# Where the weights and the rest of x are loaded around the last inverse transform: first layer's weights early, second layer's weights and x later

## The chip, the cores and the metric

The kernel runs on one core of a Trainium2 chip. The metric is the device time of one launch in microseconds (us), as the median of several runs.

A core has five engines that take their instructions from queues of their own: PE (TensorE, matmul), DVE (VectorE), ACT (ScalarE), POOL (GpSimd) and SP (SyncE, which here only issues DMAs). They meet at semaphores. Each works through its queue in order: an instruction that waits holds up everything behind it on that engine, and nothing on another one that doesn't ask for it.

## The reference

One block of a transformer with adaptive layer norm. The sequence has 2048 positions of 640 channels, everything in bf16. It is

```python
mod = (_silu(c) @ w_mod).reshape(c.shape[0], 6, 1, -1)      # sa, ca, ga, sb, cb, gb
h = _layernorm(x) * (1 + ca) + sa
x = x + ga * A(h, k, v, shift_k, ssm_k, ssm_D)              # A: q * (fftconv(shift(k) * v, ssm_k) + ...)
h = _layernorm(x) * (1 + cb) + sb
x = x + gb * B(h, w1, w2, w3, w4)
# B: h1  = gelu(layernorm(h) @ w1), its four channel quarters moved by 1, -1, 2, -2 positions
#    x1  = h + h1 @ w2
#    out = x1 + gelu(layernorm(x1) @ w3) @ w4
```

A is a long convolution over the sequence, written in the reference with a real FFT of 4096 points. w1 and w2 are 640 x 640, w3 is 640 x 1728 and w4 1728 x 640.

## The kernel before

**Stages.** The FFT is done as matmuls with tables of sines and cosines that the kernel makes itself. `stage1` and `stage2_half` transform first ssm_k and then k * v. `inverse1` (ten blocks, `h` 0 to 1 and `b` 0 to 4) multiplies the two spectra on DVE (line 678), with the real and imaginary halves of one of them swapped by a DMA beforehand (line 674), and does the first half of the way back on PE (lines 689 and 690). `inverse2` does the second half, for two or three tiles of 128 positions at a time: 32 small matmuls of 32 rows by 32 columns for each tile (line 722), then two casts from PSUM to `y_all` in the buffer `Rb` (lines 211 on ACT and 213 on DVE). There are 16 tiles, in the calls [0, 1, 2], [3, 4], [5, 6, 7], [8, 9, 10], [11, 12, 13], [14, 15]. The order of the calls on PE is not the order of the tiles.

The convolution part mixes channels and positions in such a way that all of `inverse1` must be done before `inverse2` can start. From there the work goes tile by tile:

- `chain_a` (lines 798 to 801, `square_sum` at 790 on ACT) multiplies y by the gate q, adds x and sums for the layer norm; `ln_finish` (lines 763 to 779) makes mean and reciprocal root on POOL and DVE; `chain_b` (lines 812 to 817) applies the second modulation and sums again; `chain_c` (line 785 or 655) normalises for w1, and `turn` transposes on PE (line 829) and copies back from PSUM on ACT or DVE (lines 835 and 837).
- `mm_w1` multiplies by w1 (line 875 on PE, gelu at 877 on ACT), and by 128 of its columns that were gathered in `w1x` (885, gelu at 891).
- `mm_w2` (930, addition 937 on DVE), `mm_w3` (967 and 971, gelu 978 and 980), `mm_w4` (997 and 1006, then 1029 to 1035 on DVE and the store at 1038).

The first three tiles go alone through this (`CG = [[0], [1], [2], [3, 4], ...]`), the others two by two.

`make_q` (lines 655 to 663) makes q from the layer norm of x; `ln1_stats` (600 and 601 on DVE, 608 and 609 on ACT) and `ln1_fin` (618 to 623 on POOL) its statistics. x is loaded by `x_load` (line 587), four DMAs for each group of tiles: tiles 0 to 7 early, tiles 8 to 11 and 12 to 15 in the part that is changed. `mod_half` (549, 555, 562 to 570) makes the six modulation vectors from w_mod, one half vector at a time, each with a load of 400 KB, five matmuls and one copy.

**Memory.** Buffers are used several times. The table `Gs` of the transform lies in columns 0 to 6143 of `RG`. When `stage2_half` has done its last matmul, `w1_sb` takes columns 0 to 3199, `w2_sb` 3200 to 6399 and `w1x` 6400 to 7039. Columns 6144 to 8191 are also one of the four places for the swapped spectrum (`KSY`), last used by the ninth block of `inverse1`. x's tiles 8 to 15 go to the upper half of `Ra`, which is free long before. w3 and w4 go to `T01`, which the matmuls of `inverse2` read to the end.

**Order.** Every piece of work is added to a `Planner` as a task with the regions that it reads and writes, from which its dependences follow. The costs given there have no effect any more: the list `ORDER`, written out at the top, says in which order the tasks are issued, on which engine each runs (the letter: P, A, D, G for POOL, S) and which of the four PSUM places it gets (behind the colon). A task's number is the order in which `add` was called.

**What the waits of before are.** After the first call of `inverse2` stands

```python
y0 = [("Rb", 0, D)]
```

and w1, w2 and the eight x loads all read this region: they wait for the casts of tiles 0 to 2 although they need nothing of them. For w2 there is a POOL copy of one element from tile 0 of y into `w2_sb` (line 1061) that comes first; its four pieces of 32 rows for each quarter (line 1065) and its main part (1063) then wait for this copy. The copy into `w1x` (1066, POOL) waits for w1.

In SP's queue of before, the first piece of w2 stands first and waits for the POOL copy; then an x load, the last load of w_mod, w1, three x loads, w2, and the rest. Behind these stand w3 (1082) and w4 (1079, 1080, 1084).

Of the kernel before, what the change touches and what calls it, by code (L numbers as in the profile page):

```python
# [15 lines left out]
S, D, F = 2048, 640, 1728  # L16
P = 128
NT = S // P
# [9 lines left out]
38G 88P:0 90P:1 89A 17P:2 70D 122S 71D 13G 106P:3 91A 33S 84P:0 18A 107A 74G 56G 86P:2 57G 66D 85A 75D 119S 96P:3 49G 87A 98P:0 102P:1 67D 128S 99A  # L28
125S 117P:2 103A 39G 123P:0 118D 97A 137S 82P:1 58G 131S 124D 112P:2 83A 104P:3 113D 110P:0 105A 78P:1 111D 92P:2 40A 120P:3 93A 41G 129P:0 121D 134S
79A 65G 76P:2 130D 126P:3 77A 114P:1 127D 150S 80P:0 115A 232S 100P:2 42D 138P:3 43D 101A 140P:1 139D 44A 52D 45A 51D 132P:3 81A 47S 46G 135P:2 133D  # L30
35S 53A 94P:0 54A 156S 59D 146P:3 95A 55G 153S 136D 159S 141D 108P:0 221P:2 147D 109A 142P:1 60A 222A 61D 48S 205P:3 143D 162S 199P:0 62G 206A 203P:2
200A 187P:3 204D 151P:1 188A 197P:0 63G 152D 165S 219P:2 198A 230S 201P:3 220D 223P:1 229S 202A 185P:0 224D 144P:2 186A 227P:0 145D 209P:1 228A 154P:3
210A 225P:0 155D 168S 215P:2 226A 191P:1 216D 157P:3 192A 160P:0 171S 158D 189P:2 231S 166P:1 161D 190A 211P:3 167D 207P:0 212A 148P:2 208D 64A 250S
213P:0 149D 163P:3 214A 195P:1 164D 217P:2 196A 169P:0 218D 193P:3 170A 172P:1 194D 174P:2 247S 173A 236D 366S 367G 239A 244S 176P:1 175D 234A 184D
182P:2 235A 177D 286P:3 178P:0 287A 183D 238A 278D 288P:3 284P:2 180P:1 289A 179D 285A 292P:3 181D 294P:0 293A 282P:2 295A 279D 251P:3 248P:1 283A
259S 296P:0 256S 249A 281D 290P:2 297A 245P:1 291A 300P:0 253S 280D 246A 316P:2 301A 298P:1 317A 320P:0 252D 299A 321D 308P:2 314P:3 309A 318P:1 315D
306P:0 383G 257P:2 307A 233D 272S 276G 319A 342P:0 273G 258D 275S 332P:3 343D 237G 324P:2 382S 333A 338P:1 325D 270S 328P:0 339A 277S 254P:3 274S 329A
326P:2 255D 269G 267S 340P:1 327D 263G 322P:3 266S 341A 262G 334P:0 271S 268G 323D 312P:2 335A 264S 240G 260P:1 265S 474D 313A 310P:3 465D 374S 302P:0
261D 311A 304P:2 471D 303D 336P:1 305A 375G 330P:3 337D 391G 390S 331A 348P:2 360P:0 349A 472D 356P:3 368D 352P:1 357A 358P:2 369D 353A 364P:3 361A
365D 362P:1 398S 399G 376D 359A 344P:3 370P:0 363A 466D 449S 372P:2 377D 371A 346P:1 385D 345A 406S 407G 380P:0 373A 378P:3 384D 414S 415G 381A 354P:2  # L40
393D 347A 388P:0 392D 422S 423G 355A 386P:1 379A 473D 394P:2 401D 387A 350P:3 400D 430S 431G 351A 396P:1 395A 475D 404P:3 409D 397A 402P:2 408D 438S
439G 405A 446S 417D 389A 452S 410P:1 403A 412P:3 416D 411A 450P:0 425D 420P:2 413A 424D 418P:1 421A 433D 458S 419A 426P:3 455S 428P:2 241A 432D 464G
451D 436P:1 427A 441D 447P:0 429A 440D 434P:3 437A 242D 442P:2 435A 444P:1 467D 243G 443A 477D 468D 453P:3 478D 445A 448D 456P:2 479D 454A 480P:10
469D 457A 476D 470D 518P:23 481A 482D 514G 520A 537D 511P:01 483G 538D 486S 519A 493S 558D 540G 539A 578D 461S 559D 484S 459P:2 513A 495S 579D 541G
512A 491S 524P:13 561D 460A 542D 494S 560A 515P:20 485S 563D 580A 487S 562G 581D 489S 525A 606D 543D 497S 550A 582G 564D 544A 545D 565A 609D 546G 566D
526A 583D 488S 462P:1 517A 551D 498S 567G 584D 496S 516A 547D 607D 585A 548P:0 490G 586D 549A 610D 608A 587G 553P:0 568D 611A 612D 463D 569P:2 554A
588D 613G 570D 589P:1 552D 521P:23 571D 590D 618A 555P:0 614D 535S 596P:1 556A 619D 532S 615D 530S 620D 597A 594P:0 492S 616D 531S 621A 576P:1 572D
529S 622D 617A 527S 573D 528S 595A 523D 623G 577A 534S 574P:0 533S 669D 672D 624A 627D 670D 536S 575A 628P:1 625P:3 629A 673D 598P:0 671A 626D 675G
674A 638P:3 599D 636P:1 639A 676G 601D 500D 600A 677D 681D 637A 602G 682D 683D 522A 643P:1 603D 684A 678D 604P:2 679D 640P:3 605A 644D 680A 685G
660P:2 641D 645A 686G 658P:1 661A 646D 642A 656P:2 687D 659A 690D 647G 499A 591D 688P:1 691P:3 689D 654P:0 692D 657A 648D 501G 651D 701P:3 655A 592D  # L50
652P:2 506A 649P:1 653D 699P:0 650D 505D 702A 593D 507G 630D 717P:1 631D 700A 739D 740D 503A 633D 703P:0 632D 742D 741A 743D 706P:3 718A 745D 744A
634D 723P:1 707D 502A 746G 662P:2 704D 709G 751D 708A 752D 705A 635D 753D 724A 710G 747A 754A 721P:1 663D 504G 508A 711D 714D 809D 748D 712P:2 763A
715P:0 719P:3 716D 722A 749D 713A 664D 750A 793P:2 764D 666S 693A 755D 668S 765D 789P:1 665S 756G 794A 694D 667S 509A 695D 812D 813D 791P:2 790A 510G
760D 810D 814A 815D 761P:1 792A 787P:0 762D 757D 720A 833D 834D 811A 882D 758P:3 883D 725P:21 696A 816G 759D 884A 697D 788A 698D 879D 821A 766D 880D
817A 822D 885G 771P:0 823D 769P:3 772A 818D 819D 824A 825D 726P 835D 820A 727D 881A 767D 826G 728D 770A 729S 731S 886G 827A 776P:3 732S 733D 730S 830A
768D 946D 828P:1 831P:2 777D 829A 773P:0 887A 832D 734D 841P:2 839P:3 836D 738S 842A 943D 736S 774D 737S 888D 779G 775A 944D 795P:20 891A 947D 778A
889D 948A 892D 780G 893D 840A 949D 895D 796P 781A 797D 945A 798D 890A 950G 784D 802S 894A 735S 799S 785P:2 896G 803D 782P:3 786A 843P:1 837D 783A 955D
557G 951A 804D 846P:3 956D 808S 844D 806S 861P:2 805S 847D 845A 800S 838D 848A 897D 1007D 857P:3 862A 952D 1008D 900A 1010G 849G 901P:2 898P:1 902D
863P:0 899A 953D 1009A 957D 905P:1 954A 903P:2 1011G 864A 906A 959G 1012D 1013D 859P:0 1014D 904A 850G 1016D 858A 910P:2 860A 958A 907P:0 911D 960G
851D 912A 865P:23 908D 854A 913D 909A 1015A 914G 1017G 855P:0 852P:1 856A 866P 918D 964D 853D 867D 915D 868D 871S 916P:2 921P:1 872S 917D 869S 1018D  # L60
# [4 lines left out]
1040P:0 997S 1002D 1069A 1005S 1003S 1098P:2 1041A 1004S 1042P:1 939S 1076P:0 1046P:3 1077A 1043A 1044P:0 1072P:1 1045A 1047A 1048P:30 1073A 1049P  # L65
1050D 1074P:3 1056D 1057D 1051D 1060S 1092P:0 1075A 1052S 1070P:1 1099A 1054S 1059S 1053S 1058S 1006S 1094P:2 1071A 1055S 1061S 1096P:3 1095A 1093A
1078P:21 1097A 1079P 1080D 1081D 1082S 1085S 1084S 1083S 1100P:23 1086D 1087D 1101P 1088S 1104D 1091S 1105D 1089S 1108S 1090S 1110D 1109S 1111D 1107S
1113A 1114S 1115A 1112S 1106S
"""


# [69 lines left out]
def kernel(  # L141
# [4 lines left out]
    nc = tc.nc  # L146
# [928 lines left out]
    for tl in rest:  # L1075
        inverse2(tl)
# [68 lines left out]
```

## Time and profile before

| what | value |
|---|---|
| median of 3 runs | 314.64 us (314.64, 314.64, 319.94) |
| profiled execution, its own time | 316.53 us |
| its span, first to last instruction | 314.8 us |
| busy: PE, PEld, DVE, ACT, POOL | 286.4, 222.4, 226.7, 229.7, 102.0 us |
| mean granted clock of PE | 0.966 |
| DMA moved | 32.20 MB |
| w1 (L1062), 800 KB | issued at 112.57 us, landed 7.2 us later |
| w2 (L1063), 640 KB | issued at 114.61 us, landed 9.4 us later |
| L1061, the POOL copy | 110.66 us |
| first matmul of `inverse2` (L722) / `mm_w1` (L875) / `mm_w2` (L930) / `mm_w3` (L971) | 108.44 / 124.71 / 137.47 / 147.21 us |

A line of the profile gives, from the left: start and duration in us, engine, line of the kernel, operation, output tile and input tiles, shape, count; in square brackets the idle time of the engine in front of it and what ended it. "issue" means that nothing the profile shows was waited for. Such an attribution names the latest event among those that the instruction waited for, and it can be wrong; where the named one was long over, it was another. Neighbouring instructions of one kind are drawn together in a line. Buffers appear with shortened names: RG, Ra, Rb, R (R3, R5), T (T01). `ps_...` are places in PSUM. SPq is the queue of SP, which issues DMAs.

### The profile page before, as it was taken

The numbers are of one execution on the slowest core, as the hardware profiler recorded it, in microseconds if no ns is written. First come the engines' busy times: TensorE is split into PE (matmuls) and PEld (weight loads), VectorE is DVE, ScalarE is ACT, GpSimd is POOL, SyncE is SP. The second block draws the span as 40 slices with busy tenths as digits, with TensorE's granted clock in tenths as the row PEclk, the third lists the DMA queues.
The fourth block names the chain that finished last, engine by engine and source line by source line (L and its number), as shares of the span: only waits on it lengthen the run. The fifth ranks groups of instructions, "written<-read, shape, count | busy, mean of one in ns | idle before, by whom it ended". The sixth has DMA issues, their size and how long they took to land.

```text
span 314.8 us, 8560 instructions
## 1 busy us (share of the span) xinstructions
PE 286.4 (91%) x3503; PEld 222.4 (71%) x3503; DVE 226.7 (72%) x451; ACT 229.7 (73%) x382; POOL 102.0 (32%) x242
## 2 busy tenths in 40 slices
PE   1799999989898956788999999999999999999993
PEld 1586775667787834666968877788798777886962
DVE  7998889999999999868888989785530634501233
ACT  6997869999999989889999998869355650430500
POOL 8686300018311457144735542635201030000000
PEclk9999999999999965779999999999999999999999
DMA  7978866167899379492000001000010001100101
GB/s 229 306 237 235 192 173 156 26 180 178 210 247 240 105 216 197 143 374 83 1 2 24 1 7 31 18 21 2 5 51 2 0 2 31 49 1 2 49 21 43
DMA packets 25205, 32.20 MB, mean 102 GB/s; under 512 B 2761, under 2 KB 21838, under 8 KB 25166
## 3 DMA queue, kind: packets, MB, share of 16 engines
q1 hardware_dynamic: 24030, 28.40, 32.4%
q0 software_dynamic: 1040, 3.21, 4.6%
q8 instruction: 27, 0.44, 0.6%
q14 instruction: 12, 0.10, 0.1%
q10 hardware_dynamic: 96, 0.04, 0.1%
HBM read 21.55 MB, written 2.62 MB: 77 GB/s over the span
## 4 chain that ended last, share of the span: by engine, by line
PE 70%; ACT 13%; DMA 7%; DVE 6%; issue 1%; POOL 0%; SPq 0%; DVEq 0%; ACTq 0%
PE ps_w L1006 18%; PE ps_w L971 18%; PE ps_w L930 7%; ACT T L211 6%; PE ps_w L875 5%; DMA RG<-in_B_w_dram 4%; PE ps_s L463 3%; ACT R L211 3%; PE ps_tr L829 3%; PE ps_ksh L524 3%; PE ps_tk L503 3%; PE ps_s L443 2%; DMA Ra<-in_A_k_dram 2%; PE ps_w1x L885 1%; DVE Rb L430 1%
## 5 line engine op out<-in xcount | busy, mean ns | idle before, releaser
L971 PE MATMUL ps_w<-R,T 128*128 128x256 bf16 (+1 forms) x585 | 61.2, 261 | 0.1
L1006 PE MATMUL ps_w<-T,R 128*128 128x320 bf16 x416 | 59.2, 299 | 0.0
L971 PEld LDWEIGHTS <-T 128*128 128x128 bf16 x585 | 51.3, 98 | 6.3 <-issue 0.2
L1006 PEld LDWEIGHTS <-R 128*128 128x128 bf16 x416 | 40.0, 98 | 16.1 <-issue 1.1
L980 ACT ACTIVATE R<-ps_w 128x1024 bf16<-128x1024 f32 (+2 forms) x29 | 25.3, 886 | 23.9 <-PE ps_w L971 23.6
L1029 DVE TENSOR_TENSOR T<-ps_w,R 128x640 bf16<-128x640 f32 x15 | 12.3, 821 | 34.1 <-PE ps_w L997 26.2
L211 ACT CAST T<-ps_s 128x1024 bf16<-128x1024 f32 x35 | 33.5, 1034 | 4.4 <-PE ps_s L443 4.3
L211 ACT CAST R<-ps_s 128x960 bf16<-128x960 f32 (+1 forms) x31 | 27.9, 974 | 4.6 <-PE ps_s L463 4.4
L790 ACT ACTIVATE RG<-R 128x640 bf16<-128x640 bf16 x32 | 23.5, 735 | 6.3 <-DVE R L937 5.8
L937 DVE SCALAR_TENSOR_TENSOR R<-ps_w,R 128x640 bf16<-128x640 f32 x16 | 13.0, 821 | 20.9 <-PE ps_w L930 20.9
L443 PE MATMUL ps_s<-F1bd,Rb 128*128 128x256 bf16 x160 | 22.2, 284 | 5.9 <-DVE Ra L481 4.7
L930 PE MATMUL ps_w<-RG,R 128*128 128x320 bf16 x160 | 24.7, 308 | 1.3 <-ACT R L877 1.3
L875 PE MATMUL ps_w<-R,RG 128*128 128x256 bf16 (+1 forms) x200 | 20.2, 260 | 3.6 <-ACT R L877 1.9
L443 PEld LDWEIGHTS <-Rb 128*128 128x128 bf16 x160 | 15.6, 101 | 11.0 <-DVE Ra L481 5.1
L463 PE MATMUL ps_s<-T,RG 64*128 64x160 bf16 x512 | 21.4, 230 | 1.6 <-ACT R L211 0.7
L776 POOL TENSOR_TENSOR lnv<-lnv,mhalf 128x2 f32<-128x2 f32 (+1 forms) x29 | 21.8, 752 | 2.3
L463 PEld LDWEIGHTS <-RG 64*128 64x128 bf16 x512 | 17.6, 94 | 5.5 <-issue 3.7
L930 PEld LDWEIGHTS <-R 128*128 128x128 bf16 x160 | 15.8, 101 | 7.8 <-ACT R L877 1.6
L875 PEld LDWEIGHTS <-RG 128*128 128x128 bf16 x200 | 17.3, 103 | 5.4 <-issue 4.0
L689 PE MATMUL ps_i<-EA,Rb 128*128 128x128 bf16 x160 | 19.2, 220 | 1.3 <-ACT T L211 0.7
L775 POOL TENSOR_TENSOR lnv<-stat,lnv 128x2 f32<-128x2 f32 x19 | 5.7, 300 | 45.4 <-ACT RG L790 41.9
L690 PE MATMUL ps_i<-EB,Rb 128*128 128x128 bf16 x160 | 19.1, 219 | 0.0
(198 smaller groups left out, 591.1 us busy)
## 6 DMA issues: line engine op xcount, KB each, us to landing
Ra<-in_A_ssm_k_dram SPq DMA_DIRECT2D x5, 512.0 KB, 5.9
R<-in_w_mod_dram SPq DMA_DIRECT2D x6, 400.0 KB, 5.0
out_dram<-RH SPq DMA_DIRECT2D x60, 40.0 KB, 1.6
T<-in_B_w_dram SPq DMA_DIRECT2D x5, 432.0 KB, 7.5
Ra<-in_A_k_dram SPq DMA_DIRECT2D x6, 320.0 KB, 5.0
Ra<-in_A_v_dram SPq DMA_DIRECT2D x6, 320.0 KB, 3.5
RH<-in_w_mod_dram SPq DMA_DIRECT2D x4, 400.0 KB, 4.2
Ra<-in_A_q_dram SPq DMA_DIRECT2D x4, 320.0 KB, 4.0
```

Source lines behind the costliest of these rows:

```text
L211: nc.scalar.copy(dst, src(ps.tile))
L443: nc.tensor.matmul(psv[:, ml, :], lhsT=xL[:, s0:s0 + P], rhs=F1r, start=True, stop=True)
L463: nc.tensor.matmul(psv[:, g, j], lhsT=Gs[p, k, 64 - 64 * cc:192 - 64 * cc], rhs=T1h[h][p, cc * 32 + k], start=(cc == 0), stop=(cc == 1), t ...
L689: nc.tensor.matmul(psv[:, w, :], lhsT=Av[:, r_, :, g_], rhs=EAf, start=True, stop=False)
L690: nc.tensor.matmul(psv[:, w, :], lhsT=Bv[:, r_, :, g_], rhs=EBf, start=False, stop=True)
L776: nc.gpsimd.tensor_tensor(rs, rs, mhalf[:, 0:n], ALU.pow)
L790: add("ACT", 0.74, lambda e: nc.scalar.activation(junk, src, ACT.Square, scale=float(D) ** -0.5, accum_out=stat[:, li, 1, t:t + 1]), r=[sk ...
L875: nc.tensor.matmul(pt[:, fb, 0:cw], lhsT=w1_sb[:, b, 160 * fb:160 * fb + P], rhs=hT[:, b, 0:cw], start=(b == 0), stop=(b == ND - 1))
L930: nc.tensor.matmul(pt[:, hf, 0:320], lhsT=gsf[:, fb, c0:c0 + P], rhs=w2_sb[:, fb, 320 * hf:320 * hf + 320], start=(fb == 0), stop=(fb == 4))
L971: nc.tensor.matmul(pt[:, fl, 0:cw], lhsT=w3_sb[:, b, fb * P:(fb + 1) * P], rhs=xT[:, b, 0:cw], start=(b == 0), stop=(b == ND - 1))
L980: nc.scalar.activation(g3[g % 2][:, f0:f0 + fn, 0:cw], ps.tile[:, 0:fn, 0:cw], ACT.Gelu_apprx_tanh)
L1006: nc.tensor.matmul(bank(i, hf), lhsT=gg[:, fb, i * P:(i + 1) * P], rhs=w4_sb[:, fb, 320 * hf:320 * hf + 320], start=(fb == 0 and i == 0), ...
```

## The change

- w1's load (line 1062) no longer reads `y0`. It waits only for what used its place before.
- w2's pieces, the POOL copy in front of them and the eight x loads, with the statistics of those tiles, are added after all calls of `inverse2`, and `y0` is now tile 5 of y, which is cast in the call [5, 6, 7]. The four small pieces of w2 are added before its main part.
- Since tasks are added in another sequence, numbers 483 to 526 name other tasks. `ORDER` is written out anew from its second row. Compared task by task, 64 tasks are on another engine, and neighbours have changed places everywhere; the place of the stages is the same.
- No operation is added or taken out.

```diff
     inverse2([0, 1, 2])
-    y0 = [("Rb", 0, D)]
-    add("POOL", 0.1, lambda e: nc.gpsimd.tensor_copy(w2_sb[:, 4, 0:1], y_all[:, 0, 0:1]), r=y0, w=[("RG", 3200, 6400)])
-    dma("SP", 800, lambda q: q.dma_start(w1_sb, B_w1.rearrange("(b p) n -> p b n", p=P)), r=y0, w=[("RG", 0, 3200)])
-    dma("SP", 700, lambda q: q.dma_start(w2_sb[:, 0:4, :], B_w2.rearrange("(g r) n -> r g n", g=4)[0:P]), r=y0, w=[("RG", 3200, 6400, "w2")])
-    for g in range(4):
-        dma("SP", 60, lambda q, g=g: q.dma_start(w2_sb[32 * g:32 * g + 32, 4, :], B_w2[160 * g + P:160 * g + 160, :]), r=y0, w=[("RG", 3200, 6400, "w2")])
+    dma("SP", 800, lambda q: q.dma_start(w1_sb, B_w1.rearrange("(b p) n -> p b n", p=P)), w=[("RG", 0, 3200)])
     add("POOL", 0.8, lambda e: nc.gpsimd.tensor_copy(w1x.rearrange("p b (g r) -> p b g r", g=4), w1_sb.rearrange("p b (g r) -> p b g r", g=4)[:, :, :, P:160]),
         r=[("RG", 0, 3200)], w=[("RG", 6400, 7040)])
-
-    x_load(8, 12, y0)
-    x_load(12, NT, y0)
-    ln1_all((8, 10), (10, 12), (12, 14), (14, 16))
     inverse2([3, 4])
     gs_zero()
     rest = [[5, 6, 7], [8, 9, 10], [11, 12, 13], [14, 15]]
     for tl in rest:
         inverse2(tl)
+    y0 = [("Rb", 5 * D, 6 * D)]
+    add("POOL", 0.1, lambda e: nc.gpsimd.tensor_copy(w2_sb[:, 4, 0:1], y_all[:, 5, 0:1]), r=y0, w=[("RG", 3200, 6400)])
+    for g in range(4):
+        dma("SP", 60, lambda q, g=g: q.dma_start(w2_sb[32 * g:32 * g + 32, 4, :], B_w2[160 * g + P:160 * g + 160, :]), r=y0, w=[("RG", 3200, 6400, "w2")])
+    dma("SP", 700, lambda q: q.dma_start(w2_sb[:, 0:4, :], B_w2.rearrange("(g r) n -> r g n", g=4)[0:P]), r=y0, w=[("RG", 3200, 6400, "w2")])
+    x_load(8, 12, y0)
+    x_load(12, NT, y0)
+    ln1_all((8, 10), (10, 12), (12, 14), (14, 16))
```

The places in `ORDER` that the prediction speaks of, as sequences on one engine, in words of the code (the numbers are those of the list after the change):

- SP: ..., last load of w_mod (461S), w1 (483S), one small piece of w2 (502S), x (509S, 507S, 513S, 508S), two small pieces of w2 (505S, 504S), x (511S, 514S, 510S), w2 (506S), its last small piece (503S), then w3 and w4 (531S, 536S, 528S, 529S, ...) with one x load (512S) among them.
- POOL: the copy to `w1x` (484G) stands before tile 0's first `ln_finish` (540G); the copy of one element (501G) stands behind tile 1's second (567G) and before tile 2's (587G).
- PE: the matmuls of the last w_mod half (462P) now stand before the first call of `inverse2` (480P); then the calls [0, 1, 2], [8, 9, 10], [3, 4], [5, 6, 7], a w_mod half, [14, 15], the turn of tile 0 and its `mm_w1` (553P), the turn of tile 1, tile 0's matmuls with `w1x` (555P), the call [11, 12, 13].
- ACT: between the casts of [8, 9, 10] and the first square (539A) stands the normalisation of tile 6 in `make_q` (571A), which DVE had before, later.

## The prediction

> **What bounds the kernel now.** I read the slices of the page first, then PE's timeline where the slices dip, then the queue that each dip waits for.
>
> ```profile
> PE   1799999989898956788999999999999999999993
> PEclk9999999999999965779999999999999999999999
> DMA  7978866167899379492000001000010001100101
> ```
>
> A slice is 7.87 us. From the 20th (about 148 us) PE is full to the end: the table of stretches gives 159.93 us busy of 160 from 148 to 308. So the end is set by the moment at which PE gets into that stage, and a microsecond won or lost before it is one at the end. The one hole is in slices 15 to 18, 110 to 142 us, and there PE's clock is down as well. The same stretch, cut finer:
>
> ```profile
> 108.00:112.00 4.00, 3.02 (x216) 2.26 (x215) 3.80 (x8) 3.25 (x6) 0.78 (x12) 1.00 0.04 11
> 112.00:116.00 4.00, 2.85 (x85) 1.47 (x85) 3.96 (x12) 2.90 (x7) 2.64 (x4) 0.56 0.84 251
> 116.00:120.00 4.00, 1.49 (x93) 1.03 (x85) 3.49 (x11) 3.94 (x10) 2.94 (x5) 0.50 1.10 263
> ```
>
> The columns are length, then PE, PEld, DVE, ACT, POOL busy, PE's clock, DMA share, GB/s. DVE and ACT are nearly full while PE idles: over 108 to 148 us ACT is busy 34.46 of 40 and DVE 34.53, PE only 29.22. PE waits here for the element-wise chain of the first tiles. At most 5.5 us of ACT's time in this stretch is idle, and that is about all that a better order could win.
>
> PE's timeline shows which waits these are:
>
> ```profile
> 110.92 0.38 PE L722 MATMUL ps_i<-T,RH 32*32 32x160 bf16 x20 [0.28 <-DVE Rb L213]
> 113.15 0.97 PE L722 MATMUL ps_i<-T,RH 32*32 32x160 bf16 x44 [1.85 <-issue]
> ...
> 115.50 1.46 PE L722 MATMUL ps_i<-T,RH 32*32 32x160 bf16 x79
> 119.48 1.48 PE L722 MATMUL ps_i<-T,RH 32*32 32x160 bf16 x81 [2.51 <-issue]
> ...
> 124.71 2.29 PE L875 MATMUL ps_w<-R,RG 128*128 128x128 bf16 x20 [0.78 <-DMA RG<-in_B_w_dram]
> ```
>
> The last line blames the first layer's weights. They are not it: the transfer of L1062 was issued at 112.57 and took 7.2 us, so it had landed at 119.8. What ended at the right time is ACT's copy of the turned tile 0:
>
> ```profile
> 123.97 0.69 ACT L835 COPY R<-ps_tr 128x640 bf16<-128x640 bf16 x1 [0.34 <-PE ps_tr L829]
> ```
>
> It ends at 124.66, and PE starts at 124.71. So w1 is hidden already.
>
> The two gaps "issue" are of another kind. Counted in order, the instructions in front of which PE idles are its 3,009th and 3,265th records: 256 apart. The page has a queue "q8 instruction" with 27 transfers (16 KB each in the trace) for PE's 7,006 recorded instructions. In the trace's transfers one starts at 110.26, 0.98 us after PE passed record 2,753, and PE resumes at 113.15; the next starts at 116.95, 3.79 us after record 3,009 at 113.15, and PE resumes at 119.48. The DMA share was 0.04 around the first and above 1 around the second. I read this as PE waiting for its own code, which waits among the loads of x, w1 and w2.
>
> [...]
>
> **The change, part by part.**
>
> *w1's load without its wait.* One issue (0.47 us of SP) moves from 112.57 to behind the last load of w_mod, which waits for DVE's multiplies of the ninth inverse1 block. DVE's written order puts these at about 101.7, so w1 is issued at about 102.3. The DMA engines are full to 105.2 us and idle from 106 to 110. The w_mod load (400 KB, at 264 GB/s as its neighbours moved, 1.6 us) and w1 (800 KB, at 256 GB/s, 3.2 us) end near 110. Direct worth: 0, since w1 was not waited for. The copy to w1x (POOL, 1.01 us) now stands in front of POOL's work for tile 0, which is first wanted at 112.9; a load that lands at 110 hides it. If the load took its 7.2 us after the 105.2, the copy would end at 113.4 and cost 0.5.
>
> *w2 and x held back.* In SP's queue the four small pieces of w2 and w2 itself are now mixed with seven of the eight x loads (the eighth goes among w3's), behind POOL's one-element copy (L1061), and w3 and w4 stand behind all of them. That copy needs tile 5 of y, but also its turn on POOL, where it stands behind tile 1's second normalisation. By the chain below this is at about 123.7, not 110.66. Behind it on POOL is tile 2's normalisation, not late. w2 is the eleventh issue: 10 x 0.47 = 4.7, so at 128.4. In front of it and with it are 1.9 MB; at 256 GB/s (the row 120 to 124) that is 7.5 us, so it lands at about 131.5; with the 9.4 us that it took before, at 137.8. mm_w2 is first ready at 136.5. I take 131.5: with w1 gone there is less in front of it. x's tile 9 (DVE, L600, now in front of mm_w2's addition) is wanted at 137 and lands before 134.6. w3's last piece is issued at 132.3 and lands after 4.3 MB, 2.1 of them at 380 GB/s, near 138 to 140; it is wanted near 145. All hidden, with 5 us to spare on most.
>
> *The flood leaves the inverse stage.* The second gap's wait for code falls from 6.33 us (113.15 to 119.48) to about the first's, 3.87 (109.28 to 113.15): PE is done with inverse2 some 2.4 us sooner. The first gap stays, since DMA was quiet around it. Worth on the path: only as far as ACT's queue allows.
>
> *The order.* 64 pieces of work change engine: ACT has 4 fewer, DVE 1 fewer, POOL 6 more (small ones of 0.2 to 1 us). Up to the first inverse2 the moves nearly cancel: ACT gains 8.0 us and loses 7.7 (casts of 0.97 and 1.03, copies of 1.2, statistics of 1.9), DVE -0.1. ACT and DVE are full from 80 to 108, so this stage stays as it is. DVE has 4.0 us of queue left behind its last multiply instead of 4.6, so that multiply ends 0.5 later, and inverse2 starts at 108.9, not 108.44.
>
> **The sum**, from 108.9. First inverse2 done 110.0 (half of 2.20). ACT: three casts to 112.95, the normalisation of tile 6, put in here, 0.85, square of tile 0 to 114.6 (before 113.2). POOL 0.62 + 0.58 to 115.8. DVE's L817 can follow at 116.25 (before 117.16, when two other pieces stood in front of it). ACT: squares of tiles 1 and 2, two casts of 0.65, then the second square at 117.55 (before 118.92). Then, on ACT, cast 0.95, modv 0.43, cast 0.95, cast 0.65 to 121.2, which frees the PSUM bank that tile 0's turn wants. Turn 0.7, ACT's square 0.85 and cast 0.65 to 122.7, copy 0.6: mm_w1 starts at 123.35 instead of 124.71, **1.35 sooner**. Further on: ACT's square 0.85 twice more and 0.85, table load 1.28, gelu 0.5, so w1x's gelu at 127.6 (before 130.14, when an inverse2 of 1.60 us stood in front of it); then 4 x 0.27, norm 0.85, 1.1, 0.5, two squares 1.7, 1.1, wait for POOL's pair to 135.0, norm 0.9, gelu 0.5: tile 1's gelu ends at 136.4 instead of 137.32, **0.9 sooner**. mm_w2 starts at 136.5 instead of 137.47, **1.0 sooner**. What is left over in the steady stage is between these: I take 1.2 us.
>
> The profiled execution took 316.53 us with a span of 314.8; the shown runs are 314.64, 314.64 and 319.94. The span would become 313.6, that execution 315.3, and against the median the forecast is 314.64 - 1.2 = **313.4 us**. 2% of this is 6.3 us, about what a measurement of this kernel can tell from no change.
>
> On the clock: PE's rows show 0.50 from 112.5 to 129.6 and 0.57 in 136 to 140. [...]
>
> **Rivals.** (1) *It was hidden anyway.* For it: w1 had landed 4.9 us before use, and ACT and DVE are full. Against: ACT has 1.18 us idle before 130.14 that the new order removes. Time: 314.6, to 316 if the new order's POOL work is late once. (2) *PE's clock stays up.* With the second gap gone PE may be full enough. Then mm_w1 takes 1.28 instead of 2.29, the turns 0.4 less, the inverse2 0.5, mm_w2 1.53 instead of 2.66: 3.0 us, with the 1.2 that is 310.4; all of ACT's 5.5 idle us gone, with the 0.5 late start, is 309.6, and only with both does it reach 307. Against: ACT limits most of this. (3) *The held loads come too late.* Place: SP's queue behind POOL's copy. Price: if the issues go as slowly as L1080's (3.48 us for one), w3's last piece is issued some 7 us later, at 139, and lands after its longest row, 10.8, at 150 instead of the wanted 145: 5 us, and the pause drops the clock again, 1.7 us of half speed: 314.6 + 6.7 - 1.2 = 320.1. It decides from the moment that w2 lands after 136.5 or w3 after 145. For it: twelve transfers in a row behind one small copy on a busy engine. Against: 5 us of slack by the sum above. (4) That w1 is not loaded earlier, because SP is blocked in front of it: then w1 lands near 119 again and nothing is lost; it belongs to (1).
>
> **How the numbers follow.** Forecast (312 to 314.4) 0.50; hidden anyway 0.18; clock 0.14; late loads 0.18. The likeliest's own range is 311.5 to 315, from the three readings and an error of a microsecond in the start. The range goes to 308.5 for the clock case and to 320.5 for the late loads. Faster by over 2% (under 308.3) needs most of (2) at its best, and errors of my order: 0.12. Slower by over 2% (over 320.9) needs (3) at its worst or an order that starves PE after 148: 0.18. Within: 0.70.
>
> **What would show it.** Right: w1 issued near 102 and landed by 111; L1061 near 123 to 124; a first gap "issue" of about 2 us and a second under 1; mm_w1 at 123 to 124; DMA full from 124 to 144 without PE waiting for it; PE full from 147. Wrong: L1061 after 126, PE waiting for L930 or L971 with a DMA named and no engine ending then, PE's clock at 1.00 after 116, or PE under 159 of 160 us after the hole.

## The result, and the profile after

The changed kernel takes 319.18 us (median of 317.70, 318.54, 319.82 and 320.43), the one before 315.1 beside it. The ratio is **1.0129, 95% interval 1.0101 to 1.0157**: some 4 us slower, where 1.2 us faster was forecast. By the 2% that counts as a difference it is the same; by its interval it is slower. Timed once more, beside other runs of before, the ratio was 1.0093 (1.0063 to 1.0123). The profiled execution took 318.54 us with a span of 316.8 (before 316.53 and 314.8).

The slices of the page after the change, to be laid beside those of before:

```profile
PE   1798999999899856858999999999999999999993
PEclk9999999999999975979999999999999999999999
DMA  6978864256899900699000001100010001001101
```

The hole is where it was, DMA in it has become quiet (slices 15 and 16: 0), and PE is full from the 20th slice as before. New is an 8 in PE's fourth slice, 24 to 32 us. That part of the kernel had no place in the prediction.

The stretches of 4 us answer to those of before (length, then PE, PEld, DVE, ACT, POOL busy, PE's clock, DMA share, GB/s):

```profile
108.00:112.00 4.00, 3.36 (x96) 2.77 (x97) 3.54 (x9) 4.00 (x8) 3.01 (x16) 1.00 0.46 157
112.00:116.00 4.00, 2.44 (x206) 1.91 (x188) 3.38 (x6) 3.35 (x5) 0.82 (x2) 0.82 0.03 6
116.00:120.00 4.00, 2.63 (x125) 1.78 (x114) 3.82 (x14) 3.94 (x10) 3.36 (x8) 0.50 0.02 4
```

The flood has left the inverse stage, as forecast: DMA share 0.03 and 0.02, before 0.84 and 1.10. PE's timeline after:

```profile
111.41 2.66 PE L722 MATMUL ps_i<-T,RH 32*32 32x160 bf16 x207 [0.64 <-ACT T L211]
115.52 2.09 PE L722 MATMUL ps_i<-T,RH 32*32 32x160 bf16 x128 [1.44 <-issue]
118.97 0.50 PE L722 MATMUL ps_i<-T,RH 32*32 32x160 bf16 x17 [1.37 <-issue]
...
125.30 2.29 PE L875 MATMUL ps_w<-R,RG 128*128 128x128 bf16 x20 [0.88 <-ACT R L835]
...
137.40 0.73 PE L829 MATMUL ps_tr<-RG,RK 128*128 128x128 bf16 x10 [2.77 <-ACT RK L653]
138.65 2.82 PE L930 MATMUL ps_w<-RG,R 128*128 128x320 bf16 x10 [0.52 <-DMA RG<-in_B_w_dram]
```

Both "issue" gaps are shorter in this pair of profiles (1.85 and 2.51 before). `mm_w1` is now put down to ACT's copy of the turned tile, as the prediction had read it before:

```profile
124.54 0.70 ACT L835 COPY R<-ps_tr 128x640 bf16<-128x640 bf16 x1
```

But inverse2 starts at 111.41 instead of 108.44, **2.97 us late**, and `mm_w2` and `mm_w3` (148.81 after, 147.21 before) are late too.

**Where the time goes** is best read with the start taken out. In every run PE goes over into nearly unbroken work with a group of 24 matmuls of `stage1` (L443), between 15.2 and 17.3 us; what comes before it is the arrival of the first loads and differs from run to run of one kernel. Counted from the first matmul of that group to the first matmul of each stage (us, from the trace):

| from PE's unbroken work to | before | before, profiled again | with only the loads moved (e1) | after | after, profiled again |
|---|---|---|---|---|---|
| end of the last k shift (L524) | 43.61 | 44.87 | 43.62 | 45.68 | 45.91 |
| inverse2 (L722) | 92.67 | 94.14 | 92.88 | 95.23 | 95.85 |
| mm_w1 (L875) | 108.94 | 109.88 | 109.06 | 109.12 | 109.74 |
| mm_w3 (L971) | 131.44 | 130.73 | 130.03 | 132.63 | 132.93 |
| end of the span | 299.05 | 298.26 | 297.61 | 300.65 | 300.94 |

Against the first profile of before, 2.1 us are lost in the first 44 us, inverse2 is 2.6 to 3.2 late, `mm_w1` is nearly level again (0.2 and 0.8 late), and `mm_w3` is 1.2 to 1.5 late. Behind it the loss grows by 0.4 to 0.5. The second profile of before ran at half clock in that group (it took 4.45 us there, 2.96 in the first profile), its last k shift ends 1.3 us later, and it had no second low stretch ahead of `mm_w3`; against it inverse2 is 1.1 to 1.7 late and `mm_w3` 1.9 to 2.2. A row of a single profile is good to no better than a microsecond.

The first loss, in PE's timeline after the change:

```profile
16.18 2.95 PE L443 MATMUL ps_s<-F1bd,Rb 128*128 128x256 bf16 x24
...
24.17 0.72 PE L503 MATMUL ps_tk<-RQ,Ra 128*128 128x128 bf16 x10 [0.36 <-DVE R L512]
24.73 0.60 PE L443 MATMUL ps_s<-F1bd,Rb 128*128 128x256 bf16 x4
25.84 3.62 PE L524 MATMUL ps_ksh<-R,RQ 128*128 128x512 bf16 x15 [0.51 <-ACT T L211]
...
40.86 1.42 PE L463 MATMUL ps_s<-T,RG 64*128 64x160 bf16 x36 [0.57 <-ACT R L211]
...
48.78 0.59 PE L463 MATMUL ps_s<-T,RG 64*128 64x160 bf16 x12 [0.20 <-DVE R L529]
```

Before, the same stretch has no bracket at all, and the first k shift (L524) stands earlier and alone:

```profile
15.77 2.96 PE L443 MATMUL ps_s<-F1bd,Rb 128*128 128x256 bf16 x24
...
22.14 0.72 PE L503 MATMUL ps_tk<-RQ,Ra 128*128 128x128 bf16 x10
22.70 1.89 PE L524 MATMUL ps_ksh<-R,RQ 128*128 128x512 bf16 x8
24.43 0.72 PE L503 MATMUL ps_tk<-RQ,RH 128*128 128x128 bf16 x10
```

A transposed pair (L503) takes PE 0.56 us from start to start, and its copy out of PSUM (L512) 0.82 us of DVE. The k shift, 1.89 us of PE for one PSUM place, gives the copies time to catch up; without it at this place, PE waits for the copy L512 (0.36 us) and for ACT's cast (0.51). By the trace PE idles 2.03 us between the group at 16.2 and the last k shift; before, 0.05.

### The profile page after: what moved, and what is told of

Its sections match the earlier page's. It is cut to its first block, busy times and chain, and to the rows that moved or that the text cites. A ratio compares the mean times of both kernels' runs of the same rounds, so it can differ in the third digit from the quotient of the medians.

```text
span 316.8 us, 8569 instructions
## 1 busy us (share of the span) xinstructions
PE 286.0 (90%) x3498; PEld 222.7 (70%) x3503; DVE 228.2 (72%) x442; ACT 225.1 (71%) x378; POOL 105.1 (33%) x256
## 4 chain that ended last, share of the span: by engine, by line
PE 66%; ACT 18%; DVE 6%; DMA 5%; issue 3%; POOL 1%; SPq 0%; DVEq 0%; ACTq 0%
PE ps_w L1006 17%; PE ps_w L971 17%; ACT T L211 8%; PE ps_w L930 7%; PE ps_ksh L524 6%; PE ps_w L875 4%; PE ps_s L463 4%; PE ps_tr L829 3%; DMA Ra<-in_A_k_dram 2%; ACT R L211 2%; PE ps_s L443 2%; DMA RG<-in_B_w_dram 2%; ACT RG L790 2%; DVE Rb L430 1%; PE ps_tk L503 1%
## 5 line engine op out<-in xcount | busy, mean ns | idle before, releaser
L971 PE MATMUL ps_w<-R,T 128*128 128x256 bf16 (+1 forms) x585 | 61.1, 261 | 0.0
L971 PEld LDWEIGHTS <-T 128*128 128x128 bf16 x585 | 51.3, 98 | 6.2 <-issue 0.5
L211 ACT CAST R<-ps_s 128x960 bf16<-128x960 f32 (+1 forms) x32 | 28.8, 955 | 6.4 <-PE ps_s L463 6.1
L837 DVE COPY R<-ps_tr 128x640 bf16<-128x640 bf16 x19 | 9.2, 489 | 27.3 <-PE ps_tr L829 27.3
L443 PE MATMUL ps_s<-F1bd,Rb 128*128 128x256 bf16 x160 | 23.1, 293 | 4.9 <-DVE Rb L430 4.5
L790 ACT ACTIVATE RG<-R 128x640 bf16<-128x640 bf16 x32 | 23.5, 735 | 2.9 <-DVE R L817 1.4
L443 PEld LDWEIGHTS <-Rb 128*128 128x128 bf16 x160 | 16.2, 104 | 9.8 <-DVE Rb L430 5.1
L930 PEld LDWEIGHTS <-R 128*128 128x128 bf16 x160 | 15.7, 100 | 8.7 <-ACT R L877 2.6
L463 PEld LDWEIGHTS <-RG 64*128 64x128 bf16 x512 | 17.6, 94 | 5.2 <-issue 4.1
L875 PE MATMUL ps_w<-R,RG 128*128 128x256 bf16 (+1 forms) x200 | 20.2, 260 | 1.1 <-ACT R L835 0.9
L776 POOL TENSOR_TENSOR lnv<-lnv,mhalf 128x2 f32<-128x2 f32 (+1 forms) x29 | 19.7, 680 | 2.3
L891 ACT ACTIVATE R<-ps_w1x 32x256 bf16<-32x256 f32 (+1 forms) x40 | 13.2, 331 | 8.6 <-PE ps_w1x L885 8.2
```

The lines of the kernel that those rows point to most:

```text
L211: nc.scalar.copy(dst, src(ps.tile))
L443: nc.tensor.matmul(psv[:, ml, :], lhsT=xL[:, s0:s0 + P], rhs=F1r, start=True, stop=True)
L463: nc.tensor.matmul(psv[:, g, j], lhsT=Gs[p, k, 64 - 64 * cc:192 - 64 * cc], rhs=T1h[h][p, cc * 32 + k], start=(cc == 0), stop=(cc == 1), t ...
L776: nc.gpsimd.tensor_tensor(rs, rs, mhalf[:, 0:n], ALU.pow)
L790: add("ACT", 0.74, lambda e: nc.scalar.activation(junk, src, ACT.Square, scale=float(D) ** -0.5, accum_out=stat[:, li, 1, t:t + 1]), r=[sk ...
L875: nc.tensor.matmul(pt[:, fb, 0:cw], lhsT=w1_sb[:, b, 160 * fb:160 * fb + P], rhs=hT[:, b, 0:cw], start=(b == 0), stop=(b == ND - 1))
```

## The experiments

Two theories were stated first. **Theory 1**: the order written out anew ahead of inverse2 makes the loss, and the moved loads gain something in the inverse stage. **Theory 2**: the held loads come too late, and that is the loss. ORDER below is the written list; steps of one kernel were renumbered where its order was put into the other's code. "Cut at n" means the first n steps in one order and the rest in the other.

**Loads alone, and the two halves of the order.**

```diff
 e1: code of the changed kernel; ORDER of before, except
+    last load of w_mod, w1           (right behind DVE's 18th multiply of inverse1)
+    POOL copy, w2 and x mixed        (where the change has them, one x load among w3's)
 e2: code of the changed kernel
-    ORDER, first 468 steps, new
+    ORDER, first 468 steps, of before
 e3: code of before
-    ORDER, first 448 steps, of before
+    ORDER, first 448 steps, new
 e4: as e3, cut at 229
```

e1: 

> Code of the changed kernel, but the order of before everywhere, except that w1's load (with the last load of w_mod ahead of it) and the held loads (w2, x, behind the touch on POOL) stand where the change puts them. Theory 1 (the order written out anew costs about 3 us ahead of the first inverse stage, and the moved loads gain about 2 us there and give about 1 back): 313 to 315 us, that is 0 to 2 us under before; inverse2 starts at 108.4 as before, mm_w1 within 14.5 us of it. Theory 2 (the held loads come too late, and that is the whole loss): 318 to 319.5 us.

Measured: 315.51, ratio 1.0030 (1.0015 to 1.0046), 0.9 us over before. Neither theory's number: the loads alone are not the loss, and they gain nothing. The waits of PE from 108 to 150 us say why (line that waited, who ended it; total, times, longest). Before:

```profile
PE ps_i L722 <- issue: 4.4, 2, 2.5
PE ps_tr L829 <- DVE RK L785: 0.8, 1, 0.8
```

With the loads moved:

```profile
PE ps_tr L829 <- DVE RK L785: 2.8, 1, 2.8
PE ps_i L722 <- issue: 2.7, 3, 1.4
```

PE waits 1.7 us less in the "issue" gaps and 2.0 longer for DVE's normalisation of tile 0. The same two rows in the ten profiles that have the order of before in this stage:

| | before | again | e1 | e3 | e4 | e5 | e6 | e8 | h4 | i2 |
|---|---|---|---|---|---|---|---|---|---|---|
| L722, issue | 4.4 | 3.3 | 2.7 | 5.1 | 2.7 | 3.5 | 5.2 | 5.3 | 2.2 | 3.6 |
| L829, DVE L785 | 0.8 | 1.7 | 2.8 | 0.6 | 2.9 | 1.8 | 0.2 | 0.9 | 2.6 | 1.9 |
| sum | 5.2 | 5.0 | 5.5 | 5.7 | 5.6 | 5.3 | 5.4 | 6.2 | 4.8 | 5.5 |

The gaps vary by 3 us, the sum by little more than one. What PE saves at the gaps it waits for at L785.

e2: 

> Code of the changed kernel, with the order of before up to the first inverse2 and the new order behind it. Theory 1: 313 to 315.5 us, since the 3 us lost ahead of inverse2 come back (inverse2 at 108.4 to 109). Theory 2: 318 to 319.5 us, as changed, since w2 and x are held as in the changed kernel.

Measured: 317.19, ratio 1.0080 (1.0054 to 1.0107). It gives back less than a half of the loss. The cut has a cost of its own: PE waits 0.77 us for ACT's copy of a w_mod half (L570) just ahead of inverse2, which starts 94.49 us from the unbroken work on, although its last inverse1 matmul is nearly as early as before's (it ends at 91.59, before's at 91.38).

e3: 

> Code of before with its loads where they were, and the new order up to the first inverse2 only, the order of before behind it. Theory 1: 317.5 to 318.5 us (before plus about 3), inverse2 at about 111. Theory 2: 314.5 to 315.5 us, as before.

Measured: 318.32, ratio 1.0101 (1.0064 to 1.0138), some 3.2 us over before. This is Theory 1's size. But inverse2, at 112.73 by the trace, is later than the expected 111, so this cut too has added something.

e4: 

> Code of before, the new order only in about the first 50 us (stage 1 and the k shifts), the order of before behind it. Tells where ahead of inverse2 theory 1's loss lies. If the moved k shifts that leave ACT waiting at 16 to 56 us are the cause: before plus 2 to 3 us (317 to 318). If it is the late swap and the statistics ahead of the last casts at 97 to 111 us: before plus 0 to 0.7 us (315 to 315.8).

Measured: 318.14, ratio 1.0116 (1.0096 to 1.0137), 3.7 us over before: the first 50 us are enough for a loss as large. But 1.08 us of PE's idle time, at 54.5 us, is there in neither the kernel before nor the changed one; it comes from the cut. The cut was made anew in h4.

**One k shift, and the rest of the first part.**

```diff
 e5: code and order of before
-43D 101A 140P:1 139D 44A 52D 45A 51D 132P:3 81A 47S 46G 135P:2 133D 35S 53A 94P:0 54A 156S 59D 146P:3
+43D 101A 139D 44A 52D 45A 51D 132P:3 81A 47S 46G 135P:2 133D 35S 53A 94P:0 54A 156S 59D 140P:1 146P:3
 e6: as e4, with 140P (the first k shift) back behind 101A, and places 140P:0 and 132P:1
```

e5: 

> Code and order of before, with one step moved: the first k shift (8 matmuls, 1.89 us) stands on PE behind the fourth stage-1 step instead of two steps ahead of it, where the change puts it. Theory 1a (this one move starves PE): PE then waits about 0.4 us for the k multiplier copy and 0.5 us for ACT at 22 to 25 us, where it had no gap, and this is passed on: before plus 0.5 to 1.2 us. Theory 1b (the loss is made by the other moves of the first part): before plus 0 to 0.3 us.

Measured: 316.44, ratio 1.0051 (1.0024 to 1.0079): 1.6 us, more than the expected 1.2, for one step of 1.89 us moved by some 3 us. PE's timeline has just the waits that were expected:

```profile
21.89 0.72 PE L503 MATMUL ps_tk<-RQ,Ra 128*128 128x128 bf16 x10
23.55 0.72 PE L503 MATMUL ps_tk<-RQ,RH 128*128 128x128 bf16 x10 [0.94 <-DVE R L512]
24.11 0.72 PE L503 MATMUL ps_tk<-RQ,Ra 128*128 128x128 bf16 x10
25.20 0.60 PE L443 MATMUL ps_s<-F1bd,Rb 128*128 128x256 bf16 x4 [0.37 <-ACT T L211]
```

From the unbroken work on, the last k shift ends at 45.14 instead of 43.61 and inverse2 starts at 94.46 instead of 92.67: nothing on the way takes the 1.5 us back.

e6: 

> Code of before, the new order in the first 50 us except for that one k shift, which stays where it was; the order of before behind it. Theory 1a: the rest of the loss of the new first part, before plus 2.3 to 3 us. Theory 1b: all of it, before plus 3.3 to 3.8 us. If the moves only hurt together: before plus 0 to 1 us.

Measured: 318.22, ratio 1.0108 (1.0080 to 1.0136), 3.4 us over before. It can't be read as the rest of e4: two PSUM places had to be exchanged for it, and PE waits 0.36 and 0.74 us (for DVE's copy L512) where neither kernel does, besides the 1.07 us of e4's cut. Inconclusive.

**The first part, cut cleanly.** At step 241 the two orders have done the same steps but one. h4 is e4 with this cut, h2 its counterpart in the changed kernel.

```diff
 h4: code of before
-    ORDER, first 241 steps, of before
+    ORDER, first 241 steps, new
 h2: code of the changed kernel
-    ORDER, first 241 steps, new
+    ORDER, first 241 steps, of before
```

h4: 

> The kernel before, with the new order in its first 241 steps only, cut where only one step differs. If PE's 2.0 us of idle time reach the end: before plus 1.5 to 2.2 us, against plus 3.7 in the run with the rougher cut. If DVE and ACT, full from 62 to 108 us, hide it: plus 0 to 0.7 us.

Measured: 317.91, ratio 1.0098 (1.0063 to 1.0133): 3.1 us over before, more than PE's 2.02 us of idle time. From the unbroken work on, the last k shift ends at 45.80 (before 43.61) and inverse2 starts at 95.65 (92.67). DVE and ACT, in the profile of before busy for 45.12 and 45.43 of the 46 us from 62 to 108, hide nothing of it.

h2: 

> The changed kernel with the order of before in its first 241 steps (to about 55 us), cut where only one step differs. If the first part costs what PE idles there (2.0 us) and this reaches the end: 1.5 to 2 us under the changed kernel (317 to 317.5), inverse2 1.7 us earlier. If the later stages hide it (mm_w1 was level with before's): 0 to 0.5 us under it.

Measured: 318.04, ratio 1.0089 (1.0059 to 1.0120); the changed kernel's were 1.0129 and 1.0093. What comes back is unclear: PE idles 2.05 us here too, 1.7 of them in one wait for DVE's rearrangement L430, a wait that neither kernel has at this place. An old first part ahead of a new continuation is a third order, with its own wait. So the same idle time goes with nearly the same total, but that the old first part would bring the time back was not shown.

**One step on another engine.** From 62 to 108 us ACT is full: in the table of stretches of before it is busy 21.47 of 22 us (62 to 84) and 23.96 of 24 (84 to 108). The new order gives it one more piece just there, the statistics of tile 7 (L608, L609), which DVE did before.

```diff
 i2: the kernel before
-434P:3 437A 242D 442P:2
+434P:3 437A 242A 442P:2
 i1: the changed kernel
-472D 441D 242A 465D
+472D 441D 242D 465D
```

i2: 

> The kernel before with that one step changed the other way, the statistics of tile 7 on ACT. If ACT passes it on: inverse2 starts 1 to 2 us later, before plus 0.7 to 2 us. If it is hidden: before plus 0 to 0.4 us.

Measured: 316.72, ratio 1.0059 (1.0037 to 1.0081): 1.9 us. ACT's timeline in i2 shows the piece, and behind it the last three casts of inverse1 and the w_mod copy:

```profile
102.37 2.82 ACT L211 CAST T<-ps_i 128x1024 bf16<-128x1024 f32 x3
105.06 0.76 ACT L608 ACTIVATE RQ<-Ra 128x640 bf16<-128x640 bf16 x1
...
105.94 0.74 ACT L609 ACTIVATE RQ<-Ra 128x640 bf16<-128x640 bf16 x1
...
106.68 2.82 ACT L211 CAST T<-ps_i 128x1024 bf16<-128x1024 f32 x3
```

Before, six casts run without a break up to the w_mod copy:

```profile
102.63 5.59 ACT L211 CAST T<-ps_i 128x1024 bf16<-128x1024 f32 x6
108.11 0.86 ACT L570 CAST modv<-ps_mod 128x320 bf16<-128x320 f32 x2
```

inverse2 starts at 94.30 from the unbroken work on, before and e1 at 92.67 and 92.88.

i1: 

> The changed kernel with one step on another engine: the statistics of tile 7 on DVE, as before, instead of ACT. If ACT, full up to inverse2, passes this on: the last cast of inverse1 ends 1.8 us earlier, inverse2 starts 1 to 2 us earlier, and the time is 0.7 to 2 us under the changed kernel (316.5 to 318). If DVE or the last swap's transfer sets the end of inverse1, or the stage behind hides it: 0 to 0.5 us under it.

Measured: 318.96, ratio 1.0118 (1.0085 to 1.0151), as the changed kernel. ACT now idles 1.22 and 1.29 us ahead of the last casts, because PE waits for DVE:

```profile
PE ps_i L690 <- DVE Rb L678: 1.4, 2, 1.1
```

Given back to DVE at this place, the statistics delay inverse1's last multiply instead: inverse2 starts at 97.68 from the unbroken work on, unaltered at 95.23 and 95.85. In the new order both engines are full there (after, from 84 to 108 us: DVE 23.73 and ACT 23.75 of 24), and taking one step back hands the wait to the other.

**The stage up to mm_w3.**

```diff
 e8: code and order of before
-w1's load reads y0
+w1's load reads nothing; it and the last load of w_mod stand where e1 has them
 g1: the changed kernel; SP behind the POOL copy
-one piece of w2, four x loads, two pieces, three x loads, w2, last piece, w3 ...
+w2, its four pieces, seven x loads, w3 ...
 g2: the changed kernel
+10 idle transposes ahead of tile 0's turn, 8 idle matmuls ahead of its mm_w1,
+26 idle transposes ahead of tile 4's turn, 16 idle matmuls ahead of tile 3's mm_w2
 h1: the changed kernel
-ACT: gelu L877, w1x tail L891, normalisation of tile 3 L653
+ACT: gelu L877, normalisation of tile 3 L653, w1x tail L891
-DVE: four steps of make_q, then the chain of tiles 3 and 4
+DVE: the chain of tiles 3 and 4 up to its statistics, then the four steps
 h3: h2 and h1 together
 e7: as e2 up to about 122 us, then the order of e1, with three steps of make_q
     behind the chain of tiles 3 and 4 and w2's main piece first
```

e8: 

> Code and order of before; only w1's load loses its wait and stands ahead of the inverse stage (the last load of w_mod ahead of it); w2 and x are loaded where they were. If w1 was hidden anyway: before plus or minus 0.5 us. If the loss of the run with the loads alone (plus 0.9 us) comes from the hold: here nothing of it. If it comes from w1 early: plus 0.9 us here too.

Measured: 315.11, ratio 1.0014 (0.9992 to 1.0037). w1 was hidden. That the hold alone makes e1's 0.9 us is likely, but the two intervals overlap.

g1: 

> The changed kernel with one thing different: behind the touch, SP issues the five pieces of w2 first and x's pieces after them. If w2's late landing (issue 132.4, wait of 0.5 us at mm_w2) is the loss between mm_w1 and mm_w3: mm_w2 starts 0.5 us earlier and the time is 0.5 to 1 us under the changed kernel's. If PE's wait for ACT's normalisation ahead of it decides: 0 to 0.5 us under it.

Measured: 318.81, ratio 1.0107 (1.0072 to 1.0142), while the unaltered changed kernel beside it had 1.0093. PE does not wait for w2 here, and `mm_w3` is no earlier (133.39 from the unbroken work on, 132.63 and 132.93 unaltered). The wait for L653 ahead of it is 3.00 us, unaltered 2.77 and 2.99, and the second profile of the unaltered kernel has no wait for w2 either. w2's late landing was not the loss.

g2: 

> The changed kernel with 60 idle 128x128 matmuls and transposes of the identity put where PE waits (ahead of tile 0's transposes and mm_w1, ahead of the transposes before mm_w2, ahead of the second mm_w2), whose results nobody reads. If the half clock in the hole is what the loss between mm_w1 and mm_w3 comes from: mm_w2 takes 1.53 us instead of 2.82 and mm_w3 starts 1 to 2 us earlier, 1 to 2 us under the changed kernel's time. If PE's speed doesn't matter there: the same time, or up to 1 us more for the fill itself.

Measured: 319.02, ratio 1.0117 (1.0086 to 1.0147). The clock came back (1.00 from 136 to 144 us, in the unaltered kernel beside it 0.79), the time didn't. `mm_w2` in g2, where it took 2.82 and 2.28 us unaltered:

```profile
140.05 1.52 PE L936 MATMUL ps_w<-RG,R 128*128 128x320 bf16 x10
```

It is faster by 0.8 to 1.3 us and starts 0.7 to 1.4 later, since the idle work (1.61 us) stands in front of the turns and waits with them. So what a faster PE is worth by itself is not settled by it to better than a microsecond.

h1: 

> The changed kernel with one part of its late order undone: behind the first gelu, ACT normalises tile 3 (L653, 0.92 us) before the w1x tail (L891, 1.09 us), and DVE runs the chain of tiles 3 and 4 up to its statistics before four steps of make_q (1.9 us). If this order makes the loss between mm_w1 and mm_w3: the wait of PE for L653 falls from 2.8 to 1 to 1.8 us, mm_w3 starts 1 to 2 us earlier, 1 to 2 us under the changed kernel (316.5 to 318). If not: within 0.5 us of the changed kernel.

Measured: 319.19, ratio 1.0137 (1.0101 to 1.0173). The wait was the same, and another stands behind it:

```profile
PE ps_tr L829 <- ACT RK L653: 2.8, 1, 2.8
PE ps_tr L829 <- DVE RK L655: 1.1, 1, 1.1
```

This part of the order is not the cause by itself.

h3: 

> The changed kernel with both, the old first part and tile 3 and 4's chain first. If the two make the whole loss: 314 to 315.5 us, as before. If one hides behind the other: 316 to 317.5 us.

Measured: 319.31, ratio 1.0139 (1.0106 to 1.0171). Neither answer.

e7: 

> Code of the changed kernel; the order of before up to inverse2, the new order from there to about 122 us (where it brought mm_w1 1.7 us earlier), then the order of before again, with three steps of make_q behind the two tiles' chain on DVE and the main piece of w2 issued first behind the touch. If the new order's gain at mm_w1 was lost again because DVE and ACT run make_q and the w1 tail ahead of the next two tiles' normalisation, and because w2 lands late: mm_w3 starts 1 to 2 us earlier than in the run with the loads alone, 313 to 314.5 us. If the loss lies in the held loads themselves: 315 to 317 us.

Measured: 317.02, ratio 1.0068 (1.0042 to 1.0094). `mm_w1` was the earliest of all (108.38 from the unbroken work on), and `mm_w3`, at 133.06, later than in the changed kernel. It failed as a better version: the statistics behind the chain stood behind make_q here, which was this experiment's own mistake.

**The same stage in all profiles.** Read by the order that stands behind inverse2, the traces show a gain and a loss (first matmul to first matmul, us; the changed kernel twice, e2, g1, h1, h2, h3 and i1 have the new order there; e7, which mixes the two, and g2, with its idle matmuls, are in neither column):

| | old order, ten profiles | new order, eight profiles |
|---|---|---|
| inverse2 to mm_w1 | 15.7 to 17.6 | 13.9 to 14.2 |
| mm_w1 to mm_w3 | 20.9 to 22.5 | 22.8 to 24.3 |
| inverse2 to mm_w3 | 36.6 to 39.1, median 37.2 | 36.8 to 38.2, median 37.7 |

So the loss between `mm_w1` and `mm_w3` belongs to the order behind inverse2: e2 has it too, with the old order up to there. It gives back what the new order gains up to `mm_w1`, a part of which is only work carried ahead of inverse2 (one w_mod half, five matmuls).

**The same kernels again.**

g0_before_again: 

> The kernel before, profiled once more: its profile lay 1.9 us above the median and showed the half clock from 112.5 to 129.6 us and again from 136.4 to 139.8. If the half clock makes the spread: a profile near 314.5 us has one low stretch fewer, and the stage from mm_w1 to mm_w3 takes about 22 us instead of 23.5.

Measured: 317.29 for this one execution; the runs of before beside it had a median of 315.28. Its clock was low once in the hole (116.4 to 130.0) and once at 17.4 to 20.8, and `mm_w1` to `mm_w3` took 20.85 us against 22.50 (21.8 against 23.5 counted from weight load to weight load, as the expectation does). So the profile without a second low stretch has this stage 1.7 us shorter; the slow total came from the start, where the unbroken work began at 17.34 instead of 15.77 and ran at half clock for its first 3.4 us.

g0_after_again: 

> The changed kernel, unaltered, profiled and timed beside the three below: about 1.013 of before. From the second 8-matmul group of the ssm kernel to the last k shift PE idles about 2.0 us (before 0.05), mm_w1 to mm_w3 takes about 24.5 us.

Measured: 318.40, ratio 1.0093 (1.0063 to 1.0123); idle 2.09 us, `mm_w1` to `mm_w3` 24.25 by the expectation's count (23.19 from matmul to matmul). The idle time and the stage are as expected; the ratio is lower than 1.013, and the two intervals overlap.

No kernel tried beats the one before; e8 and e1 come nearest.

## Why the prediction was wrong

**The step that failed** is the sentence "Up to the first inverse2 the moves nearly cancel", with "this stage stays as it is" behind it. Its term was 0.5 us (108.44 to 108.9); measured are 2.97 us on the clock of the profile, 2.6 and 3.2 with the start taken out (1.1 and 1.7 against the second profile of before). The old kernel with the new order ahead of inverse2 (e3), or only in its first part (e4, h4), loses 3.1 to 3.7 us, as much as the whole change, while the loads alone lose 0.9 (e1). From inverse2 to `mm_w3` the two orders take about the same (medians of 37.2 and 37.7 us), so what is late at inverse2 stays. The sum of what ACT and DVE gain and lose per engine was a sum over the whole stretch, and says nothing of when each piece is ready. Two things in the profile of before spoke against it. From 15.8 us to the last k shift PE idles 0.05 us in all, so an order that makes it wait there is paid for, as e5 and h4 show; the prediction looked at PE only from 108 us on. And ACT is busy 23.96 of 24 us from 84 to 108, so "statistics of 1.9" on ACT, which was in the list of what it gains, could not be set against casts that it loses elsewhere. e5 and i2 show both prices one by one, 1.6 and 1.9 us, each for one step of more than a thousand. That the two add up in the changed kernel was not shown: no single step taken back in it brought them back (i1), nor did the old first part (h2), which brought a wait of its own.

**w1 worth nothing**: right (e8: 1.0014, with 1 inside the interval). It was issued at 103.74 instead of the forecast 102.3, and its copy on POOL ran at 111.61, in time.

**The gaps for code**: right in direction in the first pair of profiles. The code transfer behind the first gap started 1.09 us after PE had passed its mark, 3.79 before, and the gaps were 1.44 and 1.37 us (forecast 2 and under 1). But profiled again the gaps are 1.27 and 2.00 us before and 1.32 and 2.19 after, although the transfer started 1.13 us behind its mark after and 2.94 before: an earlier transfer did not shorten the gap there. In all twenty traces the two gaps lie at the same records of PE to within six (3,003 to 3,009 and 3,259 to 3,265), whatever the order, which fits a wait for code; it was not tested by itself. After the change they take 2.81 us of PE's time with the DMA quiet (share 0.03 and 0.02 from 112 to 120 us), 4.36 before.

**Worth of the gaps**: mis-sized. "Only as far as ACT's queue allows" was the right doubt, and the 1.35 us then taken for `mm_w1` was too much. e1 has the quiet DMA in before's order, and `mm_w1` stands at 109.06 against 108.94. In the changed kernel the stage from inverse2 to `mm_w1` did shrink, 16.27 to 13.89 us where the sum had 14.45, but with a later start: a w_mod half and statistics stand ahead of inverse2 there that stood behind it before. Work had been carried over the line from which the prediction counted.

**The held loads**: the POOL copy (now L1069) came at 125.84, not 123.7. w2 was issued at 132.41, not 128.4, and took 6.1 us, so it landed at 138.5, not 131.5 and just past the bound of 137.8; PE waited 0.52 us, one of the signs that the prediction had named for being wrong. Of the 7.0 us, 2.6 are the later start (126.32), 1.4 the ten issues in front (6.1 us instead of 4.7), and 3.0 the transfer itself (6.1 instead of 3.1). w3 was in time, no DMA is named at L971.

**mm_w2 1.0 us sooner**: wrong, 1.18 later. The gelu chain on ACT that the sum followed was not what PE waited for; PE stood 2.77 us at the turn of tiles 3 and 4 for L653, where before it had waited 0.34:

```profile
136.38 1.25 PE L829 MATMUL ps_tr<-RG,RK 128*128 128x128 bf16 x10 [0.34 <-DVE RK L655]
```

The links ahead of it after the change are ACT's second square of the pair, POOL's steps and L653:

```profile
134.84 0.19 ACT L790 ACTIVATION_READ_ACCUMULATOR RG<-R 128x1 f32 x1
135.11 0.20 POOL L775 TENSOR_TENSOR lnv<-stat,lnv 128x2 f32<-128x2 f32 x1 [6.04 <-ACT RG L790]
136.16 0.23 POOL L778 TENSOR_TENSOR lnv<-lnv 128x2 f32<-128x2 f32 x1
136.42 0.92 ACT L653 ACTIVATE RK<-R,lnv 128x640 bf16<-128x640 bf16 x1 [0.39 <-POOL lnv L778]
```

From 124 to 135 us ACT idles 0.3 us there (before 1.4, h1 0.5), which may be why another order of the same pieces (h1) won nothing. What would shorten the chain stays open: its order on ACT and DVE (h1), w2 (g1) and PE's clock (g2) were changed one by one without effect.

**The rivals**: (3), late loads, gave 320.1 us and so a time near the measured one, but not for its reason, as e1 and g1 show. (2) did not happen: the clock was 0.50 from 116 to 120 us as before. That PE's pauses bring it down, as (2) and (3) suppose, no run shows by itself; g2 fits it: from 136 to 144 us the clock stood at 1.00 there, with PE busy for 6.33 us, and at 0.79 unaltered, with 5.84. (1) describes the loads well. What happened, a loss ahead of inverse2, was named in half a sentence ("an order that starves PE after 148") and at the wrong place. That the time came near that of (3) is chance.

PE's full stage came as forecast: 159.65 of 160 us from 150 to 310. The point that what is lost before it is lost at the end holds.

## What to carry to other kernels

When an order is written out anew, go through the whole timeline for the engine that has no gap in each stretch, and ask of each moved piece whether that engine now waits: a balance of busy time per engine doesn't show it. A long piece of PE's work among short ones may be what lets the copies catch up (here the k shift, 1.89 us, among pairs of 0.56), and one statistics step on a full engine can cost its whole length (1.9 us in i2). A wait that is made shorter is worth something only if nothing ends just behind it (in e1 PE waited 1.7 us less in one place and 2.0 more in the next); compare marks that no work was carried across, and take the same kind of record for both (the first matmul, not the weight load that may stand in front of it).

## What was not expected of the hardware

The low clock does not stand at fixed places. In the profile of before PE ran at half clock from 112.5 to 129.6 and from 136.4 to 139.8 us; profiled again, from 116.4 to 130.0 only, and once at 17.4 to 20.8, right behind waits for the first loads (1.07 and 1.08 us). In the last comparison the eleven runs of before with a mean granted clock of 0.976 to 0.978 have a median of 314.44 us, the five under 0.972 one of 315.48. All eight timed runs of the changed kernel lie at 0.966 to 0.973. This goes with the longer wait ahead of `mm_w2`; whether the clock is a cause of the loss or only follows it, g2 leaves open, since it held the clock at 0.974 to 0.975 and was no faster. The loss of the first part is there without it: the three runs of h4 at 0.977 to 0.978 took 316.36 to 317.95 us.
